# Moving the second token tile's load to ScalarE's queue and shortening the TensorE warm-up

## The chip, the cores and the metric

The kernel runs on one core of a Trainium2 chip. The metric is the device time of one execution in microseconds (us); less is better. The core has a matrix engine (TensorE, PE in the profile, its weight loads as PEld), a vector engine (VectorE, DVE), a scalar engine (ScalarE, ACT), GpSimd (POOL) and a sync engine (SyncE, SP) that here only issues DMAs. ACT can issue DMAs too; such an issue is shown as ACTq, one of SP as SPq. Each engine runs its instructions in the order in which they stand in its queue.

## The reference

`x` has 2048 tokens of 512 numbers in bf16. The output is `x` plus two branches on the same layer-normalised tokens.

```python
xn = _layernorm(x, axis=-1)
# A: linear attention with 32 heads of 16; phi(u) = [softmax(u @ w_phi), softmax(-u @ w_phi)] per head
q, k, v = split(xn @ wqkv)
kv = einsum("bhsf,bhsd->bhfd", phi(k), v);  z = einsum("bhsf->bhf", phi(k))
o = einsum("bhqf,bhfd->bhqd", phi(q), kv) / (einsum("bhqf,bhf->bhq", phi(q), z)[..., None] + 1e-6)
# B: two dense layers, 512 -> 1792 -> 512, with h * tanh(softplus(h)) between them
h = xn @ w1 + b1
return x + o @ wo + (h * tanh(softplus(h))) @ w2
```

## The kernel before

The tokens are cut into 16 tiles of 128, in four groups of four. All stays in on-chip memory: tokens in `x_sb`, their normalised and transposed form in `xnT`. The order of all work is written out by hand: the string `STEPS` lists steps, a table maps their names to functions, and each function appends its instructions to the engines' queues in that order. The memory dependences then decide what waits for what. DMAs of the start are issued ahead of the steps.

The start is the stretch that the change touches. Every key projection is folded with `w_phi` before use: the key half of `wqkv` is turned (`wT`) and multiplied by a block-diagonal `Wbd` made of `w_phi`. Half of the turning is done by a DMA that transposes, and half on PE. The steps involved are:

- the warm-up (L512): `WARM` matmuls of 512 columns and `SHORT` ones of 128, on constants, into a bank that nothing reads
- `TW 0`, `TW 1` (`ptw`, L569): PE turns the two row blocks of the key weights that were loaded into `wkp`; `TK` (L575): ACT copies them into `wT`
- `LS i` (L164, L166): DVE takes the statistics of token tile i; `RS i` (L170, L171): POOL makes 1/sqrt(var + eps), two instructions; `AZ i` (L175): DVE applies them, making `xn`
- `KM` (L521): a mask from constants; `WB` (L526): DVE makes `Wbd` from `wsrc`, the loaded `w_phi`
- `PB` (L535): PE turns the bias `b1b`
- `TP i` (`ptr`, L562): PE turns tile i; `TC i` (L581): it is copied to `xnT`
- `F0 kt` (`pfold`, L150): PE folds one row block; `FD kt` (L159): it is copied back into `wkp`
- `LP` (L203): key logits of tiles 0 and 1, eight matmuls, row block by row block
- `V` (`pv`), `L` (`pl`): values and logits of one tile (L188); `H` (L222): one 128-wide block of the hidden layer for a group of four tiles

Steps stand in this order at the start:

```
TW 0 @0; TW 1 @1; LS 0; LS 1; RS 0; PB @2; KM; AZ 0; TK 0 a; RS 1; DX 2; WB; TP 0 @3; F0 0 @4; AZ 1;
TP 1 @5; TK 1 a; FD 0 a; TC 0 v; F0 1 @0; F0 2 @1; FD 1 a; F0 3 @3; FD 2 a; TC 1 v; LS 2; RS 2; FD 3
v; LS 3; CB; LP i @4,5; V 1 @0; AZ 2; ...
```

The letter behind a copy names its engine (a for ACT, v for DVE), and `@` names a PSUM bank. On DVE's queue this gives: statistics of tiles 0 and 1, mask, `AZ 0`, `Wbd`, `AZ 1`, the copies of tiles 0 and 1, statistics of tile 2, the last copy of folded weights. On PE's queue `F0 0` stands ahead of `TP 1`, and the other folds behind it.

SP issues at the start, in this order: token tiles 0 and 1 (128 KB each, one DMA each), `wkp` (256 KB), the transposing load into `wT`, tiles 2 and 3 (256 KB), `wv` (512 KB), the first half of `w1` (896 KB), tiles 4 to 7 (512 KB), the second half of `w1`. ACT issues `b1b` (3.5 KB) and `wsrc` (16 KB, in pieces of 16 numbers), and then loads its activation table.

Of the kernel before, what the change touches and what calls it, by code (L numbers as in the profile page):

```python
# [19 lines left out]

WARM, SHORT = 9, 3
STEPS = """
TW 0 @0; TW 1 @1; LS 0; LS 1; RS 0; PB @2; KM; AZ 0; TK 0 a; RS 1; DX 2; WB; TP 0 @3; F0 0 @4; AZ 1;
TP 1 @5; TK 1 a; FD 0 a; TC 0 v; F0 1 @0; F0 2 @1; FD 1 a; F0 3 @3; FD 2 a; TC 1 v; LS 2; RS 2; FD 3
# [36 lines left out]
def kernel(  # L63
# [12 lines left out]
    nc = tc.nc  # L76
# [10 lines left out]
    x_v = A_x.flatten_outer_dims().rearrange("(t p) d -> p t d", p=P)  # L87
# [19 lines left out]
    x_sb = persist.tile([P, NT, D], BF16, name="x_sb")  # L107
# [365 lines left out]

    part = (slice(0, 384), slice(384, 512))

    for t in range(2):
        nc.sync.dma_start(x_sb[:, t, :], x_v[:, t, :])


    wT_of = {0: lnp.tile([P, 4, 512], BF16, name="wT", tag="xn")}  # L480
# [193 lines left out]
```

## Time and profile before

| | |
|---|---|
| median of 3 runs | 174.08 us (173.86 to 174.14) |
| profiled execution | 173.99 us |
| span in its trace, first to last instruction | 172.3 us |
| PE busy | 167.7 us, 97% |
| DVE, ACT, POOL busy | 145.1, 118.4, 9.5 us |
| HBM read, written | 7.10 MB, 2.10 MB |

Times within a trace count from its first instruction. "Idle before" names what an engine was waiting for just before an instruction. A matmul's length in the trace includes the time it takes to pass through the array; matmuls overlap, so the distance between starts is what each one costs. Times to landing count from the start of a DMA's issue to its completion.

### The profile page before, as it was taken

To read this page: it belongs to the slowest core of one execution; us is meant where nothing else is said; L and a number is where in the kernel's file an instruction comes from. 1 tells how busy PE (TensorE), PEld (TensorE's weight loads), DVE (VectorE), ACT (ScalarE), POOL (GpSimd) and SP (SyncE) were. 2 spreads that over 40 slices of the span, in tenths; PEclk is the share of its full clock that TensorE was granted. 3 is DMA by queue.
4 is the path that set the end of the run, shared out by engine and by line. 5 is a ranking of instruction groups with operands and counts; after the bars stand their busy time and mean duration, and the time that the engine had idled before them with its cause. 6 is when DMAs were issued, how large, how long until landed. Compare 5 with 4: busy or idle time off the path is not lost.

```text
span 172.3 us, 2711 instructions
## 1 busy us (share of the span) xinstructions
PE 167.7 (97%) x1031; PEld 82.9 (48%) x1047; DVE 145.1 (84%) x224; ACT 118.4 (69%) x191; POOL 9.5 (5%) x26
## 2 busy tenths in 40 slices
PE   8999999999999999999999999999999999999993
PEld 2644444444555454454444744454544444554452
DVE  3878999999689999989999899898899978884333
ACT  2637899997998999799878968966813456541200
POOL 4332203200000000000000000000000000000000
PEclk9999999999999999999999999999999999999999
DMA  4997190689910000000000443037683736868931
GB/s 131 299 373 240 27 214 5 122 142 254 344 57 0 0 4 0 0 0 4 0 0 0 83 91 73 0 63 133 97 160 101 151 83 135 155 142 204 135 101 61
DMA packets 44185, 18.02 MB, mean 105 GB/s; under 512 B 35980, under 2 KB 44172, under 8 KB 44172
## 3 DMA queue, kind: packets, MB, share of 16 engines
q1 hardware_dynamic: 43472, 17.73, 44.7%
q8 instruction: 8, 0.13, 0.4%
q10 hardware_dynamic: 700, 0.12, 0.4%
q14 instruction: 5, 0.04, 0.1%
HBM read 7.10 MB, written 2.10 MB: 53 GB/s over the span
## 4 chain that ended last, share of the span: by engine, by line
PE 91%; DVE 3%; DMA 3%; issue 1%; SPq 1%; DVEq 0%
PE ph L222 28%; PE po L456 24%; PE pl L188 14%; PE pv L188 7%; PE po L463 7%; DMA xnT<-wv 3%; PE warm L512 3%; PE pkv L380 2%; PE pnd L411 2%; PE pwide L188 1%; SPq L471 1%; PE pfold L150 1%; PE ptr L562 1%; DVE x_sb L470 1%; PE ptw L569 0%
## 5 line engine op out<-in xcount | busy, mean ns | idle before, releaser
L456 PE MATMUL po<-w_sb,acts 128*128 128x512 bf16 (+2 forms) x231 | 50.3, 366 | 0.3
L222 PE MATMUL ph<-xnT,w_sb 128*128 128x512 bf16 x224 | 49.8, 379 | 0.0
L233 ACT ACTIVATE acts<-ph,b1f 128x512 bf16<-128x512 f32 x56 | 36.2, 698 | 5.4 <-PE ph L222 5.1
L299 DVE TENSOR_REDUCE s<-e 128x128 f32<-128x2048 bf16 x16 | 36.0, 2277 | 1.7 <-ACT e L282 1.7
L222 PEld LDWEIGHTS <-w_sb 128*128 128x128 bf16 x224 | 21.7, 98 | 25.7
L456 PEld LDWEIGHTS <-acts 128*128 128x128 bf16 x238 | 22.3, 98 | 24.1
L282 ACT ACTIVATE e<-e 128x2048 bf16<-128x2048 bf16 x16 | 30.2, 1911 | 0.2 <-DVE e L266 0.2
L188 PEld LDWEIGHTS <-xnT 128*128 128x128 bf16 x184 | 17.6, 98 | 20.1
L470 DVE TENSOR_TENSOR x_sb<-po,x_sb 128x512 bf16<-128x512 f32 (+2 forms) x17 | 11.0, 656 | 8.9 <-PE po L463 8.9
L426 ACT COPY ds<-pnd 128x32 f32<-128x32 f32 x16 | 3.0, 185 | 22.0 <-PE pnd L411 22.0
L188 PE MATMUL pv<-wv,xnT 128*128 128x512 bf16 x62 | 15.7, 379 | 0.1
L246 ACT CAST p_sb<-pl 128x512 bf16<-128x512 f32 x23 | 12.9, 592 | 4.0 <-PE pl L188 4.0
L463 PE MATMUL po<-wqk,xnT 128*128 128x512 bf16 (+2 forms) x66 | 15.4, 366 | 0.3 <-DMA xnT<-wv 0.2
L188 PE MATMUL pl<-wqk,xnT 128*128 128x512 bf16 x62 | 15.0, 379 | 0.1
L164 DVE BATCH_NORM_STATS2 stats<-x_sb 128x6 f32<-128x512 bf16 x16 | 10.1, 678 | 4.2 <-DMA x_sb<-in_A_x_dram 4.2
L257 DVE TENSOR_TENSOR m<-m 128x512 bf16<-128x512 bf16 (+1 forms) x32 | 11.5, 358 | 1.1
L188 PE MATMUL pl<-wkp,xnT 128*128 128x512 bf16 x46 | 11.7, 379 | 0.1
L257 DVE TENSOR_TENSOR m<-p_sb 128x1024 bf16<-128x1024 bf16 x16 | 10.9, 682 | 0.1
L266 DVE TENSOR_TENSOR e<-p_sb,m 128x2048 bf16<-128x2048 bf16 x8 | 9.8, 1225 | 0.8 <-PE pkv L380 0.5
L266 DVE TENSOR_TENSOR e<-m,p_sb 128x2048 bf16<-128x2048 bf16 x8 | 9.8, 1225 | 0.3
L333 DVE TENSOR_TENSOR e<-e,r 128x2048 bf16<-128x2048 bf16 x8 | 9.4, 1218 | 0.4 <-ACT r L308 0.4
L138 ACT ACT_TABLE_LOAD x7 | 9.0, 1283 | 0.1
(66 smaller groups left out, 133.8 us busy)
## 6 DMA issues: line engine op xcount, KB each, us to landing
w_sb<-in_B_w_dram SPq DMA_DIRECT2D x4, 896.0 KB, 7.9
out_dram<-x_sb SPq DMA_DIRECT2D x15, 128.0 KB, 1.8
x_sb<-in_A_x_dram SPq DMA_DIRECT2D x3, 512.0 KB, 8.2
wv<-in_A_wqkv_dram SPq DMA_DIRECT2D x1, 512.0 KB, 4.4
wqk<-in_A_wo_dram SPq DMA_DIRECT2D x1, 512.0 KB, 4.3
x_sb<-in_A_x_dram SPq DMA_DIRECT2D x2, 128.0 KB, 2.1
wkp<-in_A_wqkv_dram SPq DMA_DIRECT2D x1, 256.0 KB, 3.4
x_sb<-in_A_x_dram SPq DMA_DIRECT2D x1, 256.0 KB, 3.4
```

What stands on the lines that cost most here:

```text
L164: nc.vector.bn_stats(stats[:, i, :], xs[:, i, :])
L188: nc.tensor.matmul(pp, lhsT=xnT[:, t, kt, :], rhs=w[:, kt, :], start=(kt == 0), stop=(kt == KT - 1),)
L222: nc.tensor.matmul(ph_of[u][:], lhsT=w1_sb[:, kt, f * P : (f + 1) * P], rhs=xnT[:, g * TPG : (g + 1) * TPG, kt, :], start=(kt == 0), stop= ...
L233: nc.scalar.activation(acts[:, f, g * 512 : (g + 1) * 512], ph_of.pop(u)[:], ACT.Mish, bias=b1f[:, f : f + 1])
L246: copy(p_of[s][:, i, :], pl_of.pop((s, i)))
L257: nc.vector.tensor_tensor(out=m[:], in0=src[:, :, 0:half], in1=src[:, :, half : 2 * half], op=op)
L266: nc.vector.tensor_tensor(out=e_of[s][:].rearrange("p t j l c -> p (t j) l c")[:, :, pl, :].rearrange("p t (c e o) -> p t c e o", e=8, o=2 ...
L282: nc.scalar.activation(v, v, ACT.Exp)
L299: nc.vector.reduce_sum(t[:], pair(s, k).rearrange("p t j l (c e) -> p (t j l c) e", e=16), axis=AX.X)
L456: nc.tensor.matmul(po_of[t, c.stop][:, c], lhsT=acts[:, f, t * P : (t + 1) * P], rhs=w2_sb[:, f, c], start=(f == 0), stop=False,)
L463: nc.tensor.matmul(po_of[t, c.stop][:, c], lhsT=oT_of[t // 2][:, t % 2 * 4 + j, :], rhs=wo_sb[:, j, c], start=False, stop=(j == 3),)
L470: nc.vector.tensor_tensor(out=y, in0=po_of.pop((t, c.stop))[:, c], in1=y, op=ALU.add)
```

## The change

The load of token tile 1 moves from SP's queue to ACT's, where it stands first, ahead of `b1b` and `wsrc`. On SP's queue `wkp` thereby comes second, behind tile 0, instead of third. The warm-up loses one of its nine long matmuls and one of its three short ones. The steps are the same, and on every engine the rest stands in the same order.

```diff
-WARM, SHORT = 9, 3
+WARM, SHORT = 8, 2
...
-    for t in range(2):
-        nc.sync.dma_start(x_sb[:, t, :], x_v[:, t, :])
+    nc.sync.dma_start(x_sb[:, 0, :], x_v[:, 0, :])
+    nc.scalar.dma_start(x_sb[:, 1, :], x_v[:, 1, :])
```

## The prediction

> **What bounds the kernel now.** I read the page first: the busy times and the chain that ended last.
>
> ```profile
> span 172.3 us, 2711 instructions
> PE 167.7 (97%) x1031; PEld 82.9 (48%) x1047; DVE 145.1 (84%) x224; ACT 118.4 (69%) x191; POOL 9.5 (5%) x26
> ...
> PE 91%; DVE 3%; DMA 3%; issue 1%; SPq 1%; DVEq 0%
> ```
>
> TensorE (PE) carries 91% of the chain. The change removes no useful matmul, so it can only move the moment from which PE runs without a hole. For that moment I read the chain of waits in its first 16 us, whose columns are start, length and what ran.
>
> ```profile
> 0.82 4.32 PE warm L512 x12
> 5.14 0.84 PE ptw L569 x8
> ...
> 6.43 0.37 PE pfold L150 x4
> 6.80 0.24 PE ptr L562 x4
> 7.04 0.02 issue
> 7.06 0.42 DVE xnT L581
> 7.48 0.61 DVE stats L164
> ...
> 8.30 0.59 DVE wkp L159
> 8.89 0.04 issue
> 8.93 0.59 PE pl L203 x2
> 9.52 0.86 PE pv L188 x4
> ```
>
> From 8.93 us on this stretch of the chain is PE alone. Before it, PE hands over to VectorE (DVE) once, at 7.06, when the second token tile has been turned on PE (`TP 1`) and DVE copies it out (`TC 1`). DVE then has the statistics of tile 2 and the last folded weights to do before the key logits can end. So what the change is worth is how much earlier `TP 1` can run.
>
> Then the timeline of the same stretch, for who feeds `TP 1`. Its columns are start, length, engine (a q marks a DMA issue), line, operation.
>
> ```profile
> 0.79 0.66 ACTq L485 DMA_DIRECT2D b1b<-in_B_b_dram  x1
> 0.79 0.86 SPq L477 DMA_DIRECT2D x_sb<-in_A_x_dram  x2
> ...
> 1.48 0.41 ACTq L487 DMA_DIRECT2D wsrc<-in_A_w_phi_dram  x1
> ...
> 1.70 0.43 SPq L481 DMA_DIRECT2D wkp<-in_A_wqkv_dram  x1
> ...
> 5.15 0.60 POOL L171 TENSOR_TENSOR rstd<-rstd,mhalf 128x1 f32<-128x1 f32 x1
> ...
> 5.27 0.42 DVE L526 TENSOR_TENSOR Wbd<-block,wsrc 128x512 bf16<-128x512 bf16 x1
> ...
> 5.78 0.41 DVE L175 TENSOR_SCALAR xn<-x_sb,mv,rstd 128x512 bf16<-128x512 bf16 x1
> ...
> 6.58 0.27 PEld L562 LDWEIGHTS <-xn 128*128 128x128 bf16 x4
> ```
>
> Two chains meet at `TP 1`. One is PE's: warm-up, keys' weights `wkp` (issued 1.70, 3.4 us to landing, so 5.1), `ptw` from 5.11, its copy on ScalarE (ACT) from 5.76, `pfold` from 6.40. The other is that of token tile 0: it lands 2.1 us after 0.79 and its statistics start at 2.97, then GpSimd (POOL) makes the two roots one after the other until 5.75, and DVE applies the second (`AZ 1`) from 5.78 to 6.19. `TP 1` loads at 6.58, so the second chain has 0.39 us to spare today.
>
> **The change part by part.**
>
> *Sync queue (SP).* One of two tile issues leaves: 0.86 us for the two, the next issue starting at 1.70, so 0.46 us per issue (half of 1.70 - 0.79). Every later issue of that first burst moves up by as much: `wkp` to 1.25, the transposing load of `wT`, tiles 2 and 3, `wv`, both halves of `w1`, tiles 4 to 7. `wkp` lands near 4.65 if the engines keep up. Bounds: 5.1 (no gain) and 4.61 (all of it). I take 4.65, because `x1`'s bytes are in flight earlier too and the small pieces of `wsrc` start later beside it.
>
> *Warm-up.* One 512-wide and one 128-wide matmul go. Weight loads of the long ones stand 0.43 us apart, and the three short ones with their tail end 5.14, 0.1 us apart. So 0.53 us goes and the last warm-up ends near 4.6. By itself this is worth about nothing, since `ptw` waited 0.23 us for `wkp` at its weight load; together with the earlier `wkp`, PE's chain moves up by 0.46 us. If `wkp` came no earlier, PE would sit idle for those 0.5 us and nothing would be gained or lost.
>
> *ACT queue.* It issues tile 1 at 0.79, then `b1b`, `wsrc` and the table load 0.4 to 0.7 us later (0.41 and 0.66 are its two issues). `b1b` is read first at 5.92; the table load then ends near 3.7 and ACT's first work is at 5.3: covered. `wsrc` is not: issued at 1.48 with 3.8 us to landing it lands at 5.3, just when `Wbd` starts at 5.27, and behind `Wbd` on DVE stands `AZ 1`. `Wbd` starts 0.51 us ahead of `AZ 1` (5.27, 5.78); how late that lets `wsrc` be is worked out at the sum. Bounds for its landing: 5.24 (its pieces only meet less of `wkp`) to 5.9 (0.7 later). I take 5.5: started 0.46 later, but spending less of its life beside the 256 KB of `wkp`.
>
> *Token tiles 0 and 1 side by side.* Tile 1 can land up to half a us earlier, worth nothing: its statistics start at 3.79, behind those of tile 0 on DVE, not at a landing. But tile 0 now shares the engines. The windows view has their busy share at 0.73 from 2.0 to 2.5 us and 0.89 from 2.5 to 3.0, moving 244 and 249 GB/s: tile 0's 131 KB take about 0.53 us of that. So the delay of tile 0 is between 0 and 0.53 us. I take 0.25, half: tile 1's pieces alternate with tile 0's, but part of tile 0 goes out before ACT's issue has got going. The Trainium skill, "DMA: Bandwidth & Descriptors", section "Issuing engines are not separate DMA queues", says that DMAs of all issuing engines run on the same 16 engines and interleave, so that a second issuing engine only saves issue time. That rule speaks for the delay and against any gain in bytes; by it alone the sum would keep the 0.46 us of issue time and the upper half of the delay.
>
> *The sum at `TP 1`.* PE's chain would have it at 6.63 - 0.46 = 6.17. Tile 0's chain has `AZ 1` end at 6.19 plus the delay d, and a weight load follows such an `xn` by 0.05 us (`AZ 2` ends 10.07, load 10.12). So `TP 1` starts at 6.25 + d, against 6.63: the gain is 0.38 - d. With d = 0.25: 0.13 us. `AZ 1` then starts at 6.03, and `Wbd` 0.51 ahead of it doesn't hold it up if `wsrc` lands by 5.5; each 0.1 after that costs 0.1. What was spare on tile 0's chain is used up, and that chain is late next.
>
> *After that.* `TC 1`, statistics and last fold move as one; tiles 2 and 3, which the statistics read at 7.40, are issued earlier. The logits end 0.13 earlier and PE keeps it: the value weights are read at 9.36 and 4.16 + 4.4 = 8.6 is their landing; `w1` is read at 12.18 and its first half lands before 12. The statistics of tiles 4 to 7 wait for their landing at 13.41, and their DMA is also issued 0.46 earlier. Later waits on those have covers of a few tenths, enough for 0.13.
>
> The profiled execution took 173.99 us (span 172.3, 1.7 around it) against a median of 174.08. So 173.99 - 0.13 = 173.86 there, and 174.08 - 0.13 = 173.95 on the median.
>
> **The rivals.**
>
> *Full gain.* Tile 0 isn't delayed and `wsrc` is in time: 0.38, 173.7. For it: tile 0 is first at the engines, whose share in 1.5 to 2.0 us is only 0.18. Against: 0.73 and 0.89 right after.
>
> *`wsrc` late.* Landing at 5.9, `AZ 1` runs from 6.43 to 6.84, and `TP 1` starts at 6.9 instead of 6.63: 0.27 slower, 174.35. It decides from a landing of 5.65 on, where it takes the whole gain. For it: 0.4 to 0.7 us later at issue and already the last condition of `Wbd`. Against: its partner then is no longer `wkp` in full.
>
> *The full clock comes late.* This one is clearly slower. In the trace the eight `ptw` take 219/296/314 ns (least, median, most); the first four end after 0.61 us, all eight after 0.87, and from there every 128-wide one takes 219. So PE went to its full pace within `ptw`, near 5.7 us, though the page prints PEclk 9 throughout. With 0.53 us less warm-up and a hole before `ptw`, that could come later. If it came only when the logits start (7.57), the 24 `ptr` and `pfold` matmuls would stand 0.10 instead of 0.056 apart: 24 x 0.05 = 1.2 us, less some 0.3 of holes, so 0.9 slower. If it came after the logits, eight more at 0.43 instead of 0.216 add 1.7. That is 175.0 to 176.6; it decides from about 1 us of delay, half of which is lost. Against: the first matmul still starts at 0.82 and the hole is a few tenths. The Trainium skill, "TensorE: Matmul & The Clock Gate", Part 1, has the pace follow a free-running window of about 3.4 us of activity and warns against fitting to a count of cold matmuls: by it, a hole that spoils one window costs a whole further one.
>
> *Nothing moves.* `wkp` lands where it did because the same bytes share the same engines: 174.08, with PE idle instead of warming.
>
> **How the numbers follow.** About 0.2% (0.35 us) is what a measurement here can tell from no change. Small gain as summed: 0.47. Full gain: 0.22, which I count as faster, its size being at that bound. `wsrc` late: 0.11, a third of it over the bound. Nothing moves: 0.08. Late clock: 0.12. So faster 0.22, within the bound 0.62 (0.47 + 0.08 + 0.07), slower 0.16. The range reaches from the full gain and the runs' own scatter (0.2 below the median of before) to `wsrc` late: 173.5 to 174.45, leaving out the late clock.
>
> **What would show it.** Right: `wkp`'s issue at about 1.25 and `ptw` near 4.65; statistics of tile 0 a quarter later than 2.97; `AZ 1` near 6.03; `TP 1` near 6.5; the pair of logits now at 8.93 near 8.8; from there all PE starts earlier by the same amount. Wrong: statistics still at 2.97 (full gain); `Wbd` starting behind a gap that ends with `wsrc`; `ptr` and `pfold` longer than 219 ns (late clock); a new PE wait on `w1` or on the transposes near 23 to 25 us that gives the gain back.

## The result, and the profile after

The changed kernel is slower: median 174.67 us (173.83 to 176.98, 19 runs) against 173.86 us (173.51 to 174.77, 19 runs) for the kernel before. The ratio is 1.0042, interval 1.0021 to 1.0062. The ratio leaves out two runs of the changed kernel, 176.62 and 176.98 us, as slow ones. The forecast was 173.95 us, no change or slightly faster. The profiled execution took 174.53 us, against 173.99 before.

From the page of the changed kernel, span, busy times and the chain that ended last:

```profile
span 172.8 us, 2723 instructions
PE 168.1 (97%) x1045; PEld 82.7 (48%) x1045; DVE 145.0 (84%) x224; ACT 118.6 (69%) x191; POOL 9.3 (5%) x26
...
PE 94%; DMA 3%; ACTq 1%; DVE 0%; issue 0%
```

On the page little has moved: in the chain, DVE has gone from 3% to nothing, and the 1% that SP's issues had is now 1% of ACT's. Which DMA this is, the chain of waits of the first 16 us says (start, length, what ran):

```profile
0.78 0.39 ACTq L477
...
1.20 0.67 ACTq L485
...
1.91 4.75 DMA wsrc<-in_A_w_phi_dram
...
6.68 0.44 DVE Wbd L526
...
7.16 0.38 PE pfold L150 x4
...
7.89 0.67 PE pfold L150 x12
8.56 1.83 PE pl L203 x8
10.39 0.86 PE pv L188 x4
```

Before, the warm-up and `ptw` carried this stretch. Now it is ACT's three issues, one behind the other, and then 4.75 us for the 16 KB of `wsrc`. The value matmuls enter the chain at 10.39 instead of 9.52: 0.87 us later. (A piece of the chain begins where the one before it ends; by the timeline the first of them starts at 10.23 instead of 9.36. Where such a time is given below, it is that of the chain.) The timeline shows the waits on the way (in square brackets: how long the engine stood idle, and for what):

```profile
1.73 1.32 SPq L482 DMA_TRANSPOSE wT<-in_A_wqkv_dram  x1
1.91 0.42 ACTq L487 DMA_DIRECT2D wsrc<-in_A_w_phi_dram  x1
...
3.68 0.69 DVE L164 BATCH_NORM_STATS2 stats<-x_sb 128x6 f32<-128x512 bf16 x1 [3.68 <-DMA x_sb<-in_A_x_dram]
...
4.86 0.83 PE L569 MATMUL ptw<-ident,wkp 128*128 128x128 bf16 x8 [0.24 <-DMA wkp<-in_A_wqkv_dram]
...
6.68 0.42 DVE L526 TENSOR_TENSOR Wbd<-block,wsrc 128x512 bf16<-128x512 bf16 x1 [0.66 <-DMA wsrc<-in_A_w_phi_dram]
...
7.16 0.38 PE L150 MATMUL pfold<-Wbd,wT 128*128 128x128 bf16 x4 [0.69 <-DVE Wbd L526]
```

Three things are to be seen. The part meant for the keys works: `ptw` starts at 4.86 instead of 5.11. Tile 0 comes late: its statistics start at 3.68, before at 2.97. And `wsrc` comes so late that DVE, done with `AZ 0`, waits 0.66 us, and PE behind it 0.69. In the first two lines the two issues stand the other way round than before: there `wsrc` was issued at 1.48 and `wT` at 2.17; now `wT` at 1.73 and `wsrc` at 1.91. The timeline of the kernel before has, for the issue of `wT` and the statistics of tile 0:

```profile
2.17 1.32 SPq L482 DMA_TRANSPOSE wT<-in_A_wqkv_dram  x1
...
2.97 0.69 DVE L164 BATCH_NORM_STATS2 stats<-x_sb 128x6 f32<-128x512 bf16 x1 [2.97 <-DMA x_sb<-in_A_x_dram]
```

Of the 0.87 us, 0.54 is left at the end (174.53 - 173.99). The kernel before loses the rest near its end to a wait that the later one doesn't meet. PE's timeline of the kernel before:

```profile
162.92 1.25 PE L463 MATMUL po<-wqk,xnT 128*128 128x512 bf16 x5 [0.17 <-DMA xnT<-wv]
```

and of the changed one, for the same matmuls:

```profile
163.47 0.81 PE L463 MATMUL po<-wqk,xnT 128*128 128x512 bf16 x3
```

The matmuls just ahead of these (L456) start at 161.95 and 162.82, still 0.87 apart; these start at 162.92 and 163.47, 0.55 apart. So the wait for the transposing DMA cost the kernel before 0.32.

### The profile page after: what moved, and what is told of

It is laid out like the page before. It is cut to its first block, busy times and chain, and to the rows that moved or that the text cites. A ratio compares the mean times of both kernels' runs of the same rounds, so it can differ in the third digit from the quotient of the medians.

```text
span 172.8 us, 2723 instructions
## 1 busy us (share of the span) xinstructions
PE 168.1 (97%) x1045; PEld 82.7 (48%) x1045; DVE 145.0 (84%) x224; ACT 118.6 (69%) x191; POOL 9.3 (5%) x26
## 4 chain that ended last, share of the span: by engine, by line
PE 94%; DMA 3%; ACTq 1%; DVE 0%; issue 0%
PE po L456 28%; PE ph L222 28%; PE pl L188 14%; PE po L463 8%; PE pv L188 8%; DMA wsrc<-in_A_w_phi_dram 3%; PE pnd L411 2%; PE pkv L380 2%; PE pfold L150 1%; PE pl L203 1%; PE pwide L188 1%; PE ptr L562 0%; ACTq L485 0%; DVE Wbd L526 0%; ACTq L477 0%; DVE x_sb L470 0%
## 5 line engine op out<-in xcount | busy, mean ns | idle before, releaser
L456 PE MATMUL po<-w_sb,acts 128*128 128x512 bf16 (+2 forms) x238 | 51.0, 366 | 0.0
L456 PEld LDWEIGHTS <-acts 128*128 128x128 bf16 x238 | 22.2, 98 | 24.2
L164 DVE BATCH_NORM_STATS2 stats<-x_sb 128x6 f32<-128x512 bf16 x16 | 10.1, 678 | 3.7 <-DMA x_sb<-in_A_x_dram 3.7
```

The lines of the kernel that those rows point to most:

```text
L164: nc.vector.bn_stats(stats[:, i, :], xs[:, i, :])
L456: nc.tensor.matmul(po_of[t, c.stop][:, c], lhsT=acts[:, f, t * P : (t + 1) * P], rhs=w2_sb[:, f, c], start=(f == 0), stop=False,)
```

## The experiments

My theory after the two traces: `wsrc`, now third on ACT's queue, lands late and holds `Wbd` and all behind it, because its pieces meet the transposing load of `wT`. That it is the order of the two issues is what I settled on only after two forms of this had missed (`wt_plain` and `wsrc_late_only`). The rivals: the shorter warm-up costs the time; the later issue of `wsrc` alone costs it; sharing the engines with tile 1 does. Unless it says otherwise, a diff is against the changed kernel; ratios are against the kernel before, run on the same chip.

### Each half alone

The changed queues with the old warm-up (`queue_only`):

```diff
-WARM, SHORT = 8, 2
+WARM, SHORT = 9, 3
```

> The queue move alone: tile 1 first on ACT's queue, warm-up as before (nine long, three short). Theory W (wsrc, now third on ACT's queue, lands near 6.7 and holds Wbd and all behind it) and theory T (tile 0 lands late because tile 1 is beside it): the same trace as after the whole change from the landings on: statistics of tile 0 at about 3.7, Wbd at about 6.7, the last pair of logits at about 9.8, 0.3 to 0.5% slower than before. Theory C (the shorter warm-up is what costs): no slower than before, within 0.1%.

174.87 us, 1.0061 (1.0026 to 1.0097). `wsrc`, issued 1.91, lands 5.13 later at 7.04; tile 0's statistics start at 3.62.

The old queues with the new warm-up (`warm_only`; diff against the kernel before):

```diff
-WARM, SHORT = 9, 3
+WARM, SHORT = 8, 2
```

> The shorter warm-up alone (eight long, two short), all DMAs as before. Theories W and T: PE idles about 0.5 us ahead of ptw, which still starts with the landing of wkp near 5.1; nothing else moves, the time within 0.1% of before. Theory C: slower by 0.3% or more, and runs spread over 2 us as after the change.

173.93 us, 1.0014 (0.9988 to 1.0039). `wsrc` lands at 5.3 as before. In its profiled run (174.88, one of its slowest) tiles 2 and 3 landed at 8.57 and held the logits up, so the trace says nothing on the warm-up itself. The queues alone bring the loss; the shorter warm-up alone brings none that is clear of noise, though its interval reaches up to 0.4%.

### Tile 1 elsewhere on ACT's queue

Tile 1 behind `wsrc` (`tile1_last_on_act`):

```diff
-    nc.scalar.dma_start(x_sb[:, 1, :], x_v[:, 1, :])
...
         nc.scalar.dma_start(wsrc[:], wphi_v)
+    nc.scalar.dma_start(x_sb[:, 1, :], x_v[:, 1, :])
```

> Both parts of the change, but on ACT's queue tile 1 stands third, behind b1b and wsrc. Theory W: wsrc is issued at 1.48 as before and lands near 5.2, so Wbd is not late; tile 1 is issued at 1.93, lands near 4.1, its statistics start 0.3 to 0.4 us later than 3.79, its root ends near 6.0, AZ 1 starts near 6.05 and the last pair of logits at 8.8 to 8.9: no slower than before, up to 0.1% faster. Theory T alone (any sharing by two queues makes tile 0 late): statistics of tile 0 still well after 2.97, and the logits still late by over 0.3 us.

178.43 us, 1.0258 (1.0224 to 1.0292): far off what I expected. `wsrc` did land at 4.8. But now tile 1 was the one behind `wT`, as its timeline shows:

```profile
1.71 1.32 SPq L481 DMA_TRANSPOSE wT<-in_A_wqkv_dram  x1
1.92 0.52 ACTq L487 DMA_DIRECT2D x_sb<-in_A_x_dram  x1
...
7.30 0.69 DVE L164 BATCH_NORM_STATS2 stats<-x_sb 128x6 f32<-128x512 bf16 x1 [3.35 <-DMA x_sb<-in_A_x_dram]
...
8.70 0.61 PE L562 MATMUL ptr<-ident,xn 128*128 128x128 bf16 x4 [3.85 <-DVE xn L175]
```

It took 5.36 us to land, and PE stood still for 3.85. The granted clock was then at half from 6.89 to 13.71, so part of this kernel's 4.5 us is the clock's. This is what put the order of the two issues in my mind: a different load, in the place of `wsrc`, suffered as `wsrc` had.

`wsrc` first, then tile 1, then `b1b` (`wsrc_first_on_act`):

```diff
-    nc.scalar.dma_start(x_sb[:, 1, :], x_v[:, 1, :])
...
-    nc.scalar.dma_start(b1b[:], b1_v[:, :])
...
         nc.scalar.dma_start(wsrc[:], wphi_v)
+    nc.scalar.dma_start(x_sb[:, 1, :], x_v[:, 1, :])
+    nc.scalar.dma_start(b1b[:], b1_v[:, :])
```

> Both parts of the change, but ACT's queue is wsrc, tile 1, b1b. Theory W: wsrc lands before 5, so nothing waits for it and most of the loss is gone. Theory T: tile 0 meets wsrc's and tile 1's pieces, its statistics start between 3.2 and 3.7, AZ 1 between 6.0 and 6.5, the last pair of logits between 8.8 and 9.3: between 0.1% faster and 0.2% slower than before.

174.35 us, 1.0032 (1.0011 to 1.0054), a little above what I expected. `wsrc` lands at 3.3. Tile 1, issued at 1.27 and so ahead of `wT` (1.72), lands at 4.54: 0.65 us earlier at issue than in the kernel above, 2.74 earlier at landing. Still slower than before, now because tile 1 is late: `AZ 1` starts at 6.72 behind its statistics and roots.

### Which tile, and `wsrc` second

Tile 0 on ACT's queue, tile 1 on SP's (`tiles_swapped`):

```diff
-    nc.sync.dma_start(x_sb[:, 0, :], x_v[:, 0, :])
-    nc.scalar.dma_start(x_sb[:, 1, :], x_v[:, 1, :])
+    nc.scalar.dma_start(x_sb[:, 0, :], x_v[:, 0, :])
+    nc.sync.dma_start(x_sb[:, 1, :], x_v[:, 1, :])
```

> Tile 0 on ACT's queue (first) and tile 1 on SP's (first); all else as after the change, so ACT's queue is tile 0, b1b, wsrc. After the change the tile on ACT's queue was served first and landed near 3.2, the one on SP's near 3.6. Theory W (wsrc late, because it meets the transposing load of wT): statistics of tile 0 start near 3.1 instead of 3.7, but wsrc still lands at 6.5 to 7, Wbd starts behind it and the last pair of logits stays near 9.8: as slow as after the change. Theory T (tile 0 late is what costs): the last pair near 9.0 and the time back to before.

175.04 us, 1.0064 (1.0036 to 1.0092). The profiled run was its fastest (173.73), so the trace doesn't show what the others lost: statistics from 3.37, not near 3.1, `wsrc` (behind `wT`) at 5.82. Tile 0 is late on either queue, so it isn't SP's queue that delays it.

In this kernel and in the changed one, `wsrc` ahead of `b1b` (`swapped_wsrc_second`, `wsrc_second`):

```diff
-    nc.scalar.dma_start(b1b[:], b1_v[:, :])
...
         nc.scalar.dma_start(wsrc[:], wphi_v)
+    nc.scalar.dma_start(b1b[:], b1_v[:, :])
```

> Tiles swapped as in the run beside it, and wsrc ahead of b1b, so ACT's queue is tile 0, wsrc, b1b. Theory W: wsrc is issued at 1.2, most of its pieces go out before wT's, it lands at 4.5 to 5.3; statistics of tile 0 near 3.1, AZ 1 near 5.95, the last pair of logits at 8.7 to 8.9: between 0.1% faster and no change against before. If wsrc's place in its queue doesn't matter: as slow as after the change.

> After the change, with wsrc ahead of b1b: ACT's queue is tile 1, wsrc, b1b. This leaves tile 0 late and takes most of wsrc's lateness away. wsrc lands near 5, tile 0's statistics start near 3.7, its chain sets AZ 1 near 6.5 and TP 1 near 6.95, the last pair of logits at 9.2 to 9.3: 0.1 to 0.25% slower than before. If wsrc still lands after 6.2, the queue place isn't what delays it.

174.05 us, 1.0032 (1.0006 to 1.0058), and 174.04 us, 1.0022 (0.9995 to 1.0049). `wsrc`, issued at 1.22 and 1.21 ahead of `wT`, lands at 5.4 and 5.2 and holds nothing up. What is left in the first of the two is tile 0, against my expectation of no loss: its statistics start at 3.79, and the chain of waits runs from its landing over its statistics, the roots and `AZ 1` to `TP 1`. The trace of the second is of its slowest run (175.55), and shows something else besides tile 0's statistics at 3.91. `wkp` landed at 5.31, and PE's timeline reads:

```profile
5.36 1.03 PE L569 MATMUL ptw<-ident,wkp 128*128 128x128 bf16 x8 [0.75 <-DMA wkp<-in_A_wqkv_dram]
...
6.45 0.61 PE L562 MATMUL ptr<-ident,xn 128*128 128x128 bf16 x4
...
7.70 1.49 PE L150 MATMUL pfold<-Wbd,wT 128*128 128x128 bf16 x12
```

Four `ptr` take 0.61 us (0.40 before), twelve `pfold` 1.49 (0.84), and the first logits start 0.43 apart (0.22 before; here from 10.18 on): PE is at half pace until about 10.1 us. The granted clock in the windows view reads 1.00 all the same, as it does in the kernel before while the long warm-up matmuls start 0.43 apart: this figure doesn't show a full clock that comes late.

### Is it the form of `wT`?

The transposing load is replaced by a plain copy of 256 KB in 512-byte pieces, so the folded weights hold other numbers (`wt_plain`):

```diff
-    nc.sync.dma_start_transpose(
-        out=wT_of[0][:, :, 2 * P : 4 * P], in_=A_wqkv[2 * P : 4 * P, D : 2 * D]
-    )
+    nc.sync.dma_start(wT_of[0][:, :, 2 * P : 4 * P], w1_v[:, :, 0 : 2 * P])
```

> After the change, but the load into wT doesn't transpose: the same 256 KB as a plain copy (from w1, in 512-byte pieces), so the folded weights hold other numbers; all issues stand where they were. Theory W in its narrow form (wsrc crawls because its pieces alternate with a transposing load): wsrc lands by 5.3, Wbd starts near 5.8 or at once when AZ 0 is done, the last pair of logits at 9.2 to 9.4, set by tile 0. Rival (wsrc is late because of its late issue and its 512 small pieces, whatever runs beside it): wsrc still lands after 6.2, the logits near 9.8.

176.48 us, 1.0147 (1.0115 to 1.0179); all four runs have a mean clock of 0.99, so the time tells more of the clock than of the load. `wsrc`, issued 1.92, lands at 6.83. So a load that doesn't transpose makes it as late: missed, in the form in which I held the theory.

### Later issue, or order of issue?

In the kernel before, a load of 2 KB stands ahead of `b1b`, so that `wsrc` is issued as late as in the changed kernel (`wsrc_late_only`; diff against the kernel before):

```diff
+    spare = consts.tile([16, 64], BF16, name="spare")
+    nc.scalar.dma_start(spare[:], x_v[0:16, 0, 0:64])
     nc.scalar.dma_start(b1b[:], b1_v[:, :])
```

> The kernel before, with one tiny extra load (16 x 64 numbers into a spare tile) ahead of b1b on ACT's queue, so that wsrc is issued at about 1.9 as after the change; tiles, wkp and warm-up as before. Theory W (pieces of wsrc go out one by one between the large pieces of SP's queue, so a start after SP's queue has filled lands it late): wsrc lands between 5.8 and 6.8, DVE waits for it ahead of Wbd, the last pair of logits is at 9.3 to 9.9, 0.2 to 0.5% slower than before. If moving the tile itself is needed for the loss: Wbd by 5.7 and no change.

173.67 us, 0.9991 (0.9973 to 1.0008): missed. `wsrc` is issued later, but still ahead of `wT`, and `Wbd` starts without a wait:

```profile
1.93 0.40 ACTq L489 DMA_DIRECT2D wsrc<-in_A_w_phi_dram  x1
...
2.19 1.32 SPq L482 DMA_TRANSPOSE wT<-in_A_wqkv_dram  x1
...
5.05 0.42 DVE L528 TENSOR_TENSOR Wbd<-block,wsrc 128x512 bf16<-128x512 bf16 x1
```

It lands at 5.0. So 0.45 us later at issue costs nothing by itself.

Two such loads put its issue behind `wT`'s (`wsrc_behind_wt`; against the kernel before):

```diff
+    spare = consts.tile([16, 128], BF16, name="spare")
+    nc.scalar.dma_start(spare[:, 0:64], x_v[0:16, 0, 0:64])
+    nc.scalar.dma_start(spare[:, 64:128], x_v[0:16, 0, 64:128])
     nc.scalar.dma_start(b1b[:], b1_v[:, :])
```

> The kernel before with two tiny extra loads ahead of b1b on ACT's queue, so that wsrc is issued near 2.35, just after SP has begun to issue wT at 2.17; with one extra load (issue at 1.93, ahead of wT) it landed at 5.0. Theory O (what counts is whether wsrc stands ahead of or behind SP's third load): it lands near 6.5 or later, over 1 us later for an issue 0.4 us later, Wbd waits for it, the first hidden-layer matmul is at 13.0 or later instead of 12.4, and the time is 0.3 to 0.6% above before. Rival (the landing follows the issue): it lands near 5.4, Wbd waits for at most 0.2 us, no change.

174.38 us, 1.0025 (1.0005 to 1.0045). Its chain of waits:

```profile
2.40 4.19 DMA wsrc<-in_A_w_phi_dram
...
6.61 0.43 DVE Wbd L529
```

`wT` was issued at 2.18. For 0.47 us at issue `wsrc` lands 1.6 us later than in the kernel above, and the value matmuls start at 10.32, nearly as in the changed kernel. The tiles are where they were before, and statistics start at 2.89: the late `wsrc` alone.

The other way round, in the changed kernel one such load on SP's queue ahead of `wT` (`wt_behind_wsrc`), with the changed kernel once more on the same chip (`after_again`):

```diff
+    spare = consts.tile([16, 64], BF16, name="spare")
+    nc.sync.dma_start(spare[:], x_v[0:16, 0, 0:64])
     nc.sync.dma_start_transpose(
```

> The whole change, with one tiny extra load on SP's queue ahead of wT, so that wT's issue starts near 2.15, behind wsrc's at 1.91. Theory O: wsrc lands by 5.5 though it is issued when it was, Wbd hardly waits, the rest of the loss is that of tile 0 (statistics at 3.4 to 3.7): first hidden-layer matmul at 12.4 to 12.8, 0 to 0.2% above before. Rival (it is the tile's own 128 KB ahead of wsrc on ACT's queue): wsrc still lands after 6 and the time stays 0.4% or more above before.

> The changed kernel once more, beside the others: wsrc lands at 5.8 to 7, statistics of tile 0 at 3.3 to 3.7, first hidden-layer matmul near 13.2, 0.3 to 0.6% above before.

174.08 us, 1.0024 (1.0002 to 1.0047), against 176.36 us, 1.0139 (1.0098 to 1.0181), for the changed kernel, far above the 0.3 to 0.6% that I expected of it: on this chip, 2.3 us gained by a load that nobody needs. Its timeline:

```profile
1.93 0.40 ACTq L489 DMA_DIRECT2D wsrc<-in_A_w_phi_dram  x1
...
2.23 1.32 SPq L484 DMA_TRANSPOSE wT<-in_A_wqkv_dram  x1
...
5.58 0.42 DVE L528 TENSOR_TENSOR Wbd<-block,wsrc 128x512 bf16<-128x512 bf16 x1
```

`wsrc` is issued when it was in the changed kernel, lands 3.6 us later at 5.5, and `Wbd` starts without a wait. The value matmuls start at 9.73. What holds them now is not tile 0: the chain of waits runs over SP's issues to the landing of tiles 2 and 3 at 7.58 and the statistics of tile 2 at 7.60 (7.40 before). On that chip the changed kernel's own trace has `wsrc` landing 6.01 us after its issue, at 7.93. Its windows view (the columns behind each stretch: length, busy time and count for PE, PEld, DVE, ACT, POOL, then the granted clock, DMA share, GB/s):

```profile
5.22:8.64 3.42, 1.15 (x16) 0.84 (x14) 1.45 (x7) 1.07 (x2) 1.27 (x3) 1.00 1.14 204
8.64:12.05 3.41, 3.41 (x24) 2.30 (x22) 2.93 (x8) 1.66 (x3) 0.79 (x2) 0.50 1.07 370
```

PE was busy for 1.15 us of the first stretch, and through the whole of the next it runs at half clock. In the chain of waits twelve `pfold` take 1.28 us (0.67 in the first trace of the changed kernel), the logits 2.48 (1.83); with the two groups ahead of them (0.05 and 0.16) that is 1.47 us on top of the 1.28 by which PE's first fold starts later (8.44 against 7.16).

### Filling PE's holes

The old warm-up, and 15 more short matmuls on constants in the two holes (`holes_filled`):

```diff
-WARM, SHORT = 8, 2
+WARM, SHORT = 9, 3
...
-WB; TP 0 @3; F0 0 @4; AZ 1;
+WB; AW; AW; AW; AW; AW; TP 0 @3; AW; AW; AW; AW; AW; AW; AW; AW; AW; AW; F0 0 @4; AZ 1;
```

> The queue move with the old warm-up (nine long, three short), and further warm-up matmuls of 128 columns where PE stood idle: five ahead of the turn of tile 0, ten ahead of the first fold. Theory C in its new form (a hole on PE makes the full clock open late or close for a window of about 3.4 us in some executions; it adds 1 to 2 us to those): the body of the runs stays where the queue move alone had it, 174.3 to 174.9, because wsrc is as late, but the runs over 176 go away. If the holes don't matter for the clock, a quarter of the runs still lies at 176 to 178.

175.61 us, 1.0132 (1.0101 to 1.0164): missed, as the body lies higher than in `queue_only`, and two of the six are still over 176. No run shows a mean clock of 0.99. The fillers stand on PE's chain themselves (0.51 and 0.58 us), with the value matmuls at 10.38, as in the changed kernel; the traced run loses a further 0.8 us near its end, where the chain waits for a transposing DMA (`qT`) and the matmuls that stand at 158.37 in the changed kernel start at 159.13. It doesn't tell what the holes cost.

### Looking for a better kernel

`wsrc` ahead of `b1b` with the tiles on SP's queue and the short warm-up (`wsrc_first_only`; against the kernel before):

```diff
-WARM, SHORT = 9, 3
+WARM, SHORT = 8, 2
...
-    nc.scalar.dma_start(b1b[:], b1_v[:, :])
...
         nc.scalar.dma_start(wsrc[:], wphi_v)
+    nc.scalar.dma_start(b1b[:], b1_v[:, :])
```

> The kernel before with the two small loads of ACT's queue exchanged (wsrc, then b1b) and the shorter warm-up (eight long, two short); all tiles on SP's queue as before. Theory W: wsrc goes out while SP's queue is still starting and is out of wkp's way, so wkp lands near 4.6 instead of 5.1 without having moved in its queue; tile 0 meets wsrc's pieces and its statistics start 0.1 to 0.2 us late; AZ 1 near 5.9, TP 1 near 6.35, the last pair of logits near 8.7: 0.1 to 0.15% faster than before. If wkp still lands at 5.1, no change.

174.80 us, 1.0059 (1.0036 to 1.0082): missed. `wsrc` lands at 3.3, but `wkp` no earlier (5.2), and tiles 2 and 3 at 8.11, where the chain now passes. Why they came later stays open.

The spare load of `wsrc_late_only` with one long warm-up matmul fewer (`late_and_8_3`; against `wsrc_late_only`):

```diff
-WARM, SHORT = 9, 3
+WARM, SHORT = 8, 3
```

> The variant with one tiny extra load ahead of b1b (tiles on SP's queue), where wkp landed at 4.75, with one long warm-up matmul less (eight long, three short), so that PE is free when wkp lands. If wkp lands at 4.75 again: PE's chain 0.3 us earlier than before, bounded by tile 0's chain, first hidden-layer matmul near 12.1, 0.1 to 0.2% faster than before. If 4.75 was one lucky landing: within 0.1% of before.

173.69 us, 0.9988 (0.9971 to 1.0005). No kernel here is measurably faster than the one before.

## Why the prediction was wrong, step by step

*What bounds.* Right: the end follows the moment from which PE runs without a hole, and nothing else of the change shows at the end but the 0.32 us above.

*SP's issues, `wkp`, warm-up.* `wkp` was issued at 1.24 and landed at 4.8, within the bounds and 0.15 later than taken. The shorter warm-up by itself moved the time by nothing clear of noise, but it leaves a hole ahead of `ptw` (0.62 us in `warm_only`).

*The delay of tile 0.* Mis-sized: 0.71 us, where I took 0.25 with an upper bound of 0.53. Over the kernels with one tile first on each queue it was between 0.35 and 0.94, counted from the 2.97 of the kernel before (with both tiles on SP's queue the statistics started at 2.79 to 3.17). The bound counted only the bytes of one other tile. With a tile on ACT's queue but behind `wsrc`, and `wkp` directly behind tile 0 on SP's, the statistics started at 3.03 and 3.12, so it is the other tile alongside that delays, not `wkp` alone. The formula held: the gain at `TP 1` was to be 0.38 - d. In `wt_behind_wsrc`, where `wsrc` was in time, d was 3.32 - 2.97 = 0.35 and PE turned tile 1 at 6.61 instead of 6.63. In `swapped_wsrc_second` d was 0.82 and `TP 1` at 7.07, a loss of 0.44, as the formula has it. With 0.71 it gives a loss of 0.33, so this step alone would have turned the sign. The kernels with `wsrc` in time stayed 0.2 to 0.3% slower, not all by tile 0: in `wt_behind_wsrc` it was the landing of tiles 2 and 3.

*`wsrc`: the step that failed.* I took its landing at 5.5, at most 5.9, by adding the later issue to the old landing and taking off a little for less of `wkp` beside it. It landed at 6.66, and 7.93 on the other chip. What I had not looked at is the order between the two queues: the change moves `wsrc` back by 0.43 and `wT` forward by 0.44, and so past each other. All kernels by that order, one trace each:

| `wsrc` against `wT` | issue of `wsrc`, `wT` (us) | landing |
|---|---|---|
| ahead: before | 1.48, 2.17 | 5.3 |
| ahead: `warm_only` | 1.47, 2.17 | 5.3 |
| ahead: `wsrc_late_only` | 1.93, 2.19 | 5.0 |
| ahead: `late_and_8_3` | 1.92, 2.18 | 5.1 |
| ahead: `wt_behind_wsrc` | 1.93, 2.23 | 5.5 |
| ahead: `wsrc_second` | 1.21, 1.74 | 5.2 |
| ahead: `swapped_wsrc_second` | 1.22, 1.71 | 5.4 |
| ahead: `tile1_last_on_act` | 1.48, 1.71 | 4.8 |
| ahead: `wsrc_first_on_act` | 0.78, 1.72 | 3.3 |
| ahead: `wsrc_first_only` | 0.78, 2.18 | 3.3 |
| behind: after | 1.91, 1.73 | 6.7 |
| behind: `after_again` | 1.92, 1.74 | 7.9 |
| behind: `queue_only` | 1.91, 1.74 | 7.0 |
| behind: `wt_plain` | 1.92, 1.70 | 6.8 |
| behind: `holes_filled` | 1.93, 1.71 | 6.4 |
| behind: `wsrc_behind_wt` | 2.40, 2.18 | 6.6 |
| behind: `tiles_swapped`, its fastest run | 1.91, 1.74 | 5.8 |

The rival "`wsrc` late" had the mechanism and its place, from the wait of `Wbd` to `AZ 1` and PE; its price was worked out for 5.9. By its own rule, `AZ 1` 0.53 behind the start of `Wbd`, a landing of 6.66 gives about 1.0 us; the trace has 0.86 at `TP 1` (7.49 against 6.63), as `AZ 1`, whose root was ready, started 0.35 behind `Wbd`.

The Trainium skill, "DMA: Bandwidth & Descriptors", section "Issuing engines are not separate DMA queues", says that a second issuing engine saves only issue time. The runs agree in so far as `wkp`, issued 0.46 earlier, landed 0.3 earlier and brought nothing at the end; but here the second queue also changed which load stood behind which, and in the first trace that was the larger part: 0.33 us would have been tile 0's, and `wsrc` made 0.87 of it.

*The full clock.* I gave it 0.12 and a range of 175.0 to 176.6, outside my own. The first profiled run doesn't show it: full clock through PE's holes. But four of the changed kernel's 19 runs and three of the six on the other chip have a mean clock of 0.99, and they took 175.67 to 177.39; no run of the kernel before beside the experiments does. Half clock for one stretch of 3.41 us in 173 gives just 0.99. So this rival is true of some runs, and in `after_again` by way of the late `wsrc`: PE's hole let the clock fall again. In its own form, a clock that comes late, it is seen in `wsrc_second`: half pace until about 10.1 us and 175.55, where its kernel's median is 174.04, with `wsrc` in time and a hole of 0.75 us ahead of `ptw`. That this hole was the reason is not shown. The Trainium skill, "TensorE: Matmul & The Clock Gate", Part 1, gives a window of 3413 ns; the trace's stretch of half clock, 8.64 to 12.05, agrees.

*What stays open.* Why a small load issued just behind `wT` lands later is not shown; only that at the same issue time (1.91 to 1.93) it lands at 5.8 to 7.9 behind `wT` and at 5.0 to 5.5 ahead of it, and that `wT` need not transpose for that. All issues tried lie at least 0.17 us behind or 0.23 ahead, so whether the order itself decides or a steep slope between them is open too. Some runs above 176 us have a mean clock of 1.0, and no trace of such a run of the changed kernel was taken; a clock that comes late would not show in that figure. How the loss splits between the late `wsrc`, tile 0 and the clock differs from run to run and from chip to chip.

## What to carry to other kernels

Moving one load to a second queue moves every other load on both, so before pricing it, write down the issue times of both queues merged, and look for pairs that change places: here the small load that another engine waited for had to be issued ahead of the large one. A time to landing holds only for the neighbours that it was measured among. And where PE waits in its first microseconds, price the clock too.

## What the runs showed of the hardware

A spare 2 KB load on SP's queue, which put the issue of `wT` behind that of `wsrc`, made the changed kernel 2.3 us faster on one chip, half clock in three of its six runs included.

The granted clock falls after a stretch in which PE does something, not only after an idle one: 1.15 us of 3.42 busy in `after_again`, 1.38 in `tile1_last_on_act` and 1.71 of 3.41 in `wt_plain` were followed by half clock, while 2.46 of 3.42 in the first trace of the changed kernel was not. The full clock can also come late: in `wsrc_second` PE was at half pace until about 10.1 us, in the kernel before until about 5.7, and the listed clock reads 1.00 in both.

Two tiles of 128 KB issued within 0.01 us on two queues made tile 0 0.35 to 0.94 us later, with either of them on ACT's queue.
